# The instruction order of a two-attention kernel taken from a written list, a query tile turned by TensorE, and small sums moved to GpSimd

## The chip, the core and the metric

The kernel runs on one core of one Trainium2 chip. A core has five engines that run side by side: TensorE (PE in the profile; its weight loads are a row of their own, PEld), VectorE (DVE), ScalarE (ACT), GpSimd (POOL) and SyncE (SP), which here only issues DMAs. Each engine works through its own instructions in the order in which the program was written, and waits on semaphores where it needs another one's result. The metric is the device time of one execution in microseconds (us).

## The reference, cut to what matters

Two attention layers over 2048 tokens of width 640, 32 heads of 20; their outputs stand side by side (1280 columns).

```python
# A: four segments of 512 tokens, one after the other
for s in range(4):
    logits = einsum('bhqd,bhkd->bhqk', qs, ks) * scale + mask     # causal in the segment
    a_dot  = softmax(logits) @ vs
    pq     = phi(qs)                       # t+1 where t>0, else exp(t)
    a_mem  = (pq @ M) / (pq @ z + 1e-6)    # M, z: memory of the earlier segments
    o      = g * a_mem + (1 - g) * a_dot
    pk = phi(ks);  M += pk^T vs;  z += sum(pk)
a = concat(o) @ wo
# B: causal sliding window of 256 tokens over the same length
p = softmax(where((i - j >= 0) & (i - j < 256), q k^T * scale, -1e9))
b = (p @ v) @ wo
return concat([a, b], -1)
```

## The kernel before

The work is cut into eight chunks of 512 tokens, taken alternately: A0, B0, A1, B1, A2, B2, A3, B3. For each chunk the projections q, k, v come first (`qk_job`, `v_job`): groups of five matmuls over the 128x128 array ("wide" matmuls, helper `wide`, L870), 512 or 320 columns each, summed in one of only two PSUM banks, `m0` and `m1`. When a group is done VectorE copies it to SBUF (L501, L677, L682, L1027) and the bank is free again. Scores are made in batches (`score_batch`, L758): four heads at a time in 32-row strips of the array (the profile shows 20x128 operands), or in 32x64 pieces for half blocks; a batch fills two of three "sc" buffers of 128x1024. ScalarE then takes two exponentials per batch (L774, `pt<-sc`), which turns logits into weights; 306 of them are the bulk of its work, 18 more make phi (L521). GpSimd zeroes what the causal or window mask forbids (L813), VectorE does it for the half blocks (L791).

When the weights of a group of heads are ready, `av` (L827) or, in the last chunk, `av_tile` (L848: one tile of 128 queries, 16 heads) multiplies them with v, in 128x32 column strips, four matmuls at a time. VectorE transposes the result (`turn`, L883), and `norm` divides by the sum column: a reciprocal on VectorE (L908), a product on GpSimd (L918). For the memory term of A there is a sum with 1e-6 on VectorE first (L903, in place L906), and VectorE adds the product to `o` (L931). `final` stores `o` to DRAM with four DMAs (L949), reads it back transposed by a DMA (L968), and `final_job` multiplies it with `wo`, copies it and stores the output. Only the last query tile of the last chunk goes another way: `last_job` turns it by eight short steps of TensorE against a unit matrix (L1049, L1061), so without the trip through DRAM.

The order of all this is decided while the program is written. `Flow` keeps an estimate of when each engine is free; the main loop in `body` asks in turn whether the next score batch may go (`room`, `may_wait`), then the next attention-times-v or memory group (`pend`), then the next step of a projection (`jobs`, `fins`), takes the first that is ready by the estimate, and moves its clock on if none is. `room` holds back groups of many short matmuls once 160 of them were sent within 3000 ns of its clock. What comes out is a fixed order for each engine; nothing is decided on the chip.

Three kinds of array shape alternate on TensorE: whole array (wide), row strips (scores), column strips (attention times v).

Of the kernel before, what the change touches and what calls it, by code (L numbers as in the profile page):

```python
# [13 lines left out]
P = 128  # L14
# [14 lines left out]
FETCH = 160  # L29
FETCH_NS = 3000  # L30
BACK = 800.0
NTT = 4
QPOOL = 750.0
GAP = 48
# [20 lines left out]
LEAD = 500.0  # L55

# [11 lines left out]
class Flow:  # L68
# [3 lines left out]
    def __init__(self):  # L72
        self.pe = self.act = self.dve = self.pool = 0.0
        self.mode = None
        self.sp = self.fabric = 0.0
        self.landed = []
        self.bank_free = [0.0, 0.0]
        self.open = False
        self.left = 0
        self.later = []  # L80
        self.idle_dve = []
        self.idle_low = []
        self.blocked = []
        self.loads = []
        self.seq = 0
        self.load = {}
        self.slow = {}
        self.issued = []
# [11 lines left out]
    def room(self, n):  # L100


        while self.issued and self.issued[0][0] <= self.pe - FETCH_NS:
            self.issued.pop(0)
        have = n + sum(k for _, k in self.issued)
        t = self.pe
        for t0, k in self.issued:
            if have <= FETCH:
                break
            have -= k  # L110
            t = t0 + FETCH_NS
        return t

    def on_pe(self, mode, ns, cols, ready=0.0, n=1):
        self.issued.append((max(self.pe, ready), n))
        return self.on_pe_(mode, ns, cols, ready)
# [22 lines left out]
    def on_dve(self, ns, ready=0.0):  # L139
        self.dve = max(self.dve, ready) + ns  # L140
        return self.dve + 138.0

    def on_pool(self, ns, ready=0.0):
        self.pool = max(self.pool, ready) + ns
        return self.pool + 98.0
# [68 lines left out]
class _K:  # L214
# [29 lines left out]
    def warm_up(self):  # L244

        f = self.f
# [222 lines left out]
    def qk_job(self, n, what, pieces, w_ap, dst, needs, scratch, phi=None):  # L469
# [6 lines left out]
        if what == "k" and self.chunks[n][0] == "B":  # L476
            at = SH
            c = self.chunks[n][1]
            if 0 in pieces and c > 0:
                def prefix(t0):  # L480
                    nc.vector.tensor_copy(out=dst[:, :, 0:SH],
                                          in_=self.kB[(c - 1) % 2][:, :, L:L + SH])
                    f.on_dve(290.0)
                f.blocked.append((0.0, self.known(n - 2, "k", G - 1), prefix))
# [27 lines left out]
    def phi(self, in_, t, m, use):  # L512
# [13 lines left out]
        def one(in_, e, es, m, ta):  # L526
            box = []

            def s1():
                r = out(m)  # L530
                if r is None:
                    r, slot = self.piece("r", 1, 1)
                    box.append(slot)
                    r = r[:]
                box.append(r)
                nc.vector.tensor_scalar(out=r, in0=in_, scalar1=0.0, scalar2=1.0,  # L536
                                        op0=ALU.max, op1=ALU.add)
                f.on_dve(300.0, t)

            def s2():  # L540
                r = box[-1]
                nc.vector.tensor_tensor(out=r if len(box) == 1 else e, in0=r, in1=e, op=ALU.min)  # L542
                td = f.on_dve(370.0, ta)
# [60 lines left out]
    def dm_job(self, seg, pkT, v):  # L604
# [12 lines left out]
        for some in (own, [(lambda kt, h=h: spare[:, kt, R2 * h:R2 * h + R2], R2,  # L617
# [6 lines left out]
            for lhs, rows, xs, g0 in some:  # L624

                gs = [g0] if g0 is not None else sorted(MEM2[x][1] for x in xs)
                n = W * len(gs)
                v0 = at_head(4 * gs[0])
                for kt in range(LT):
                    nc.tensor.matmul(dM[0:rows, at:at + n], lhsT=lhs(kt),  # L630
                                     rhs=v[:, kt, v0:v0 + n],
                                     start=(kt == 0), stop=(kt == LT - 1))
                f.on_pe("full", 4 * mm_ns(n), 4 * n)
                at += n
                if (rows, xs) != (some[-1][1], some[-1][2]):
                    yield 0.0
# [148 lines left out]
    def mask(self, m, pt, te, ready, x):  # L785
        nc, f = self.nc, self.f
        kind, c0, n = m
        if kind == "ends":
            def go():
# [6 lines left out]
                ready[x] = f.on_dve(72.0 + 1.036 * n, te)  # L796
# [71 lines left out]
    def wide(self, ps, lhsT, rhs, n, start, stop):  # L868

        self.nc.tensor.matmul(ps[:, 0:n], lhsT=lhsT, rhs=rhs, start=start, stop=stop)  # L870
        self.f.on_pe("full", mm_ns(n), n)
# [16 lines left out]
    def norm(self, turned, dst, add_to, last, g=None):  # L888
# [12 lines left out]
        def s1():  # L901
            if add_to:
                nc.vector.tensor_single_scalar(out=rr[:], in_=tv[:, :, DH], scalar=EPS,  # L903
                                               op=ALU.add)
                f.on_dve(100.0, t0)
                nc.vector.reciprocal(out=rr[:], in_=rr[:])  # L906
            else:
                nc.vector.reciprocal(out=rr[:], in_=tv[:, :, DH])  # L908
            t1 = f.on_dve(276.0, t0)
            f.at(t1 - 100.0, lambda: s2(t1))  # L910

        def s2(t1):
# [14 lines left out]
            def add():  # L927
# [4 lines left out]
                t3 = f.on_dve(300.0, t2)  # L932
# [6 lines left out]
        f.when_idle(t0, s1)  # L939

    def final(self, n, o, scr, wo, out2d, r0, col, t0, t1, t):
# [19 lines left out]
        def turn(tl):  # L961
            if n not in self.oT:
# [3 lines left out]
                else:  # L966
# [7 lines left out]
                                                 lambda: box.get("t"))))  # L974

    def final_job(self, n, wo, out2d, r0, col, t0, t1, there):
# [4 lines left out]
        for tt in range(t0, t1):  # L981
            if n == len(self.chunks) - 1 and tt == LT - 2:

                row = r0 + tt * P
                for hf in range(2):
                    yield "bank"
                    self.last_half(hf, lambda m: oT[:, m, tt * P:(tt + 1) * P], wo,
                                   out2d[row:row + P], col)
                continue
# [46 lines left out]
    def last_job(self, o, wo, out2d, r0, col, t):  # L1036
# [4 lines left out]
        yield self.sc_free[-NSC]  # L1041
# [3 lines left out]
        b0 = LT * (LT - 1)  # L1045
# [6 lines left out]
        oT = [self.pq[:, 0, 0:4 * P], self.pkT[:, 0, 0:P]]  # L1052
# [12 lines left out]
        f.on_pe("col", 150.0, 128)  # L1065
# [5 lines left out]
        row = r0 + (LT - 1) * P  # L1071
# [93 lines left out]
    def job(self, gen):  # L1165
        return [gen, next(gen)]
# [29 lines left out]
    def seed(self, n):  # L1196
# [7 lines left out]
        add = lambda gen: self.jobs.append(self.job(gen))  # L1204
# [5 lines left out]
        else:  # L1210
            add(self.dm_job(c - 1, self.pkT, self.vA))
# [7 lines left out]
        for half, pieces in enumerate(((0, 1, 2), (3, 4))):  # L1219
            for some in ([(m,) for m in pieces] if first else [pieces]):  # L1220
                for what, w, dst, phi in qk:
                    need = [tx, gate] + ([self.known("wB" + what, some[0])] if first else [])
                    add(self.qk_job(n, what, some, w, dst, need, self.scr[what + kind][c], phi))
                if first and some[0] == AT:
                    add(self.late_v())
            if first:
                v[3] = v[3] + [self.known("wBv", half)]
            add(self.v_job(n, half, *v))

    def body(self, xA, A_wq, A_wk, A_wv, A_wo, A_beta, xB, B_wqkv, B_wo, out2d):  # L1230
# [84 lines left out]
        def first(what, m, dst, phi):  # L1315
# [3 lines left out]
                                     scr[what + "A"][0], phi)))  # L1319
        for m in range(KT):  # L1320
# [4 lines left out]
            if m == 1:  # L1325
                add(self.job(v(0)))
        self.late_v = lambda: v(1)
        if AT < 0:
            add(self.job(v(1)))
# [3 lines left out]
        pend = []  # L1333
# [6 lines left out]
        late = [(19500.0, self.zero_end), (45000.0, self.consts_e), (60000.0, self.consts_one)]  # L1340
        while True:
# [3 lines left out]
            if i < len(bs):  # L1345
                n, ent, ms, complete = bs[i]
                kind, c = chunks[n]
                if self.ring("pt", NPT) is not None:
# [4 lines left out]
                    if None not in need:  # L1353
                        t = max(need + [f.room(4 * len(ent)) if ent[0][1][0] in "lust" else 0.0])
                        if t <= f.pe and not self.may_wait():
# [12 lines left out]
                            for g in complete:  # L1368
                                pend.append((n, g, "tile" if n == NC - 1 else "av"))
                                if kind == "A" and c > 0:  # L1370
                                    pend.append((n, g, "mem"))
# [6 lines left out]
            if pend:  # L1378
# [6 lines left out]
                elif what == "av":  # L1385
                    ps_ = parts[(n, g)]
                    need = [whole(p[6] for p in ps_), self.done.get((n, "v", g))]
                else:
                    need = [self.done.get(("dm", c - 1)),
                            self.done.get((n, "pq", g) if g < KT else (n, "pq2"))]  # L1390
                if None not in need and not (f.open and 0 < f.left <= 3):
                    t = max(need + [min(f.bank_free), f.room(
                        4 * len(ps_)) if what != "mem" else 0.0])
                    wait = (f.mode == "full" and soon is not None and len(pend) < 3
                            and soon < f.pe + 2200.0 and self.more(f.pe))
                    if t <= f.pe and not wait:
                        pend.pop(0)
                        self.one_group(n, kind, c, g, what, parts, left, o_t, groups_done,
                                       scro, wo, out2d)
# [3 lines left out]
            for x, jb in enumerate(self.jobs + self.fins):  # L1403
                if f.open and not jb[0] is self.opener:
                    continue
# [7 lines left out]
            if hit is not None:  # L1413
                self.at_job = hit
                jb = (self.jobs + self.fins)[hit]
                if jb[1] == "bank":
                    f.open = True
                    self.opener = jb[0]
                try:
                    jb[1] = next(jb[0])  # L1420
                except StopIteration:
                    (self.jobs if jb in self.jobs else self.fins).remove(jb)
                while late and f.pe > late[0][0]:
# [15 lines left out]
        assert i == len(bs) and not pend and not self.jobs and not self.fins  # L1439
# [14 lines left out]
    def one_group(self, n, kind, c, g, what, parts, left, o_t, groups_done, scro, wo, out2d):  # L1454
# [22 lines left out]
        if what == "tile":  # L1477
# [19 lines left out]
        if what == "av":  # L1497
# [5 lines left out]
            if nm == 2:  # L1503
                self.norm(tt, o[:, :, DH * g:DH * (g + 1)], False, None)
                return
# [92 lines left out]
```

## Time and profile before

| | |
|---|---|
| median of 3 runs | 334.47 us (334.11 to 336.25) |
| the profiled execution | 334.4 us; its span from first to last instruction 331.6 us |
| granted TensorE clock | 1.000 |
| PE busy | 315.6 us (95%) |
| ACT busy | 302.4 us (91%) |
| DVE busy | 264.2 us (80%) |
| POOL busy | 256.3 us (77%) |
| first exponential starts, last one ends | 9.10 us, 318.27 us |

The span is counted by the profiler; the 2.8 us between it and the execution's time lie around the program. Matmuls overlap each other and their ends are modelled, so PE's share overstates how full it is; an engine's start-to-start times say more. ACT instructions overlap by about 0.1 us as well: four exponentials of 1024 columns that follow each other without a wait take 3.77 us, and one takes 1.02, so the next starts 0.917 us after the one before.

### The profile page before, as it was taken

The numbers are of one execution on the slowest core, as the hardware profiler recorded it, in microseconds if no ns is written. First come the engines' busy times: TensorE is split into PE (matmuls) and PEld (weight loads), VectorE is DVE, ScalarE is ACT, GpSimd is POOL, SyncE is SP. The second block draws the span as 40 slices with busy tenths as digits, with TensorE's granted clock in tenths as the row PEclk, the third lists the DMA queues.
The fourth block names the chain that finished last, engine by engine and source line by source line (L and its number), as shares of the span: only waits on it lengthen the run. The fifth ranks groups of instructions, "written<-read, shape, count | busy, mean of one in ns | idle before, by whom it ended". The sixth has DMA issues, their size and how long they took to land.

```text
span 331.6 us, 15794 instructions
## 1 busy us (share of the span) xinstructions
PE 315.6 (95%) x6583; PEld 174.4 (53%) x6619; DVE 264.2 (80%) x556; ACT 302.4 (91%) x333; POOL 256.3 (77%) x648
## 2 busy tenths in 40 slices
PE   8999999999999999989999999999999999999896
PEld 3444546455444455546644545455654545666564
DVE  6777767798978899989868898888667889876654
ACT  1979999999999999999999999989999999999841
POOL 8366689998659799975867879996875969977750
DMA  6975746566596852335699145044555154769852
GB/s 198 396 253 152 173 135 125 136 175 176 132 226 132 165 155 63 67 86 122 183 208 181 42 94 156 3 104 80 148 140 114 21 150 122 166 142 187 178 127 100
DMA packets 76260, 47.36 MB, mean 143 GB/s; under 512 B 48381, under 2 KB 73181, under 8 KB 76189
## 3 DMA queue, kind: packets, MB, share of 16 engines
q1 hardware_dynamic: 75469, 45.71, 56.7%
q8 instruction: 51, 0.84, 1.1%
q10 hardware_dynamic: 720, 0.66, 0.7%
q14 instruction: 20, 0.16, 0.2%
HBM read 17.62 MB, written 16.96 MB: 104 GB/s over the span
## 4 chain that ended last, share of the span: by engine, by line
PE 57%; DVE 15%; ACT 10%; issue 7%; POOL 6%; DMA 3%; SPq 1%; ACTq 0%; DVEq 0%; POOLq 0%
PE m L870 36%; PE sc L758 11%; ACT pt L774 10%; PE m L827 6%; POOL pt L813 4%; DVE pt L791 4%; PE m L848 2%; DVE tt L883 2%; POOL u L918 2%; DVE pq L542 2%; DVE kA L501 2%; DVE vA L677 1%; DMA xT<-in_A_x_dram 1%; DVE pq L536 1%; DVE ot L1027 1%
## 5 line engine op out<-in xcount | busy, mean ns | idle before, releaser
L774 ACT ACTIVATE pt<-sc 128x1024 bf16<-128x1024 f32 (+2 forms) x306 | 285.0, 1012 | 10.7 <-PE sc L758 8.6
L813 POOL TENSOR_SCALAR_AFFINE_SELECT pt<-pt 128x128 bf16<-128x128 bf16 (+1 forms) x512 | 177.1, 374 | 60.4 <-ACT pt L774 57.4
L883 DVE STREAM_TRANSPOSE tt<-m 128x512 f32<-128x512 f32 x88 | 61.4, 711 | 20.0 <-PE m L827 9.1
L918 POOL TENSOR_TENSOR o<-tt,rr 128x320 bf16<-128x320 f32 x64 | 47.8, 747 | 4.1 <-DVE rr L908 4.0
L870 PEld LDWEIGHTS <-xT 128*128 128x128 bf16 x350 | 32.0, 97 | 24.2 <-issue 12.3
L758 PE MATMUL sc<-qB,kB 20*64 20x64 bf16 (+2 forms) x1728 | 38.6, 218 | 1.4 <-issue 0.8
L791 DVE TENSOR_TENSOR pt<-pt,ends 128x1024 bf16<-128x1024 bf16 (+2 forms) x50 | 36.3, 740 | 0.0
L758 PEld LDWEIGHTS <-kB 20*64 20x64 bf16 (+1 forms) x1728 | 21.7, 98 | 23.3 <-issue 22.0
L758 PE MATMUL sc<-qA,kA 20*64 20x64 bf16 (+4 forms) x1024 | 33.1, 237 | 0.5
L1027 DVE CAST ot<-m 128x320 bf16<-128x320 f32 x56 | 26.9, 485 | 7.4 <-PE m L870 7.1
L870 PEld LDWEIGHTS <-oT 128*128 128x128 bf16 x280 | 24.7, 98 | 11.4 <-issue 1.1
L870 PE MATMUL m<-wBv,xT 128*128 128x320 bf16 x160 | 27.0, 299 | 2.4 <-DVE tt L883 2.3
L870 PE MATMUL m<-wv_A,xT 128*128 128x320 bf16 x160 | 26.0, 299 | 2.0 <-DVE vA L677 1.9
L870 PE MATMUL m<-xT,wBq 128*128 128x512 bf16 x96 | 26.4, 381 | 0.4 <-issue 0.2
L870 PE MATMUL m<-xT,wq_A 128*128 128x512 bf16 x88 | 25.0, 381 | 1.8 <-DVE vA L677 0.8
L870 PE MATMUL m<-xT,wk_A 128*128 128x512 bf16 x96 | 25.6, 388 | 1.1 <-DVE qA L501 0.7
L870 PE MATMUL m<-xT,wBk 128*128 128x512 bf16 x84 | 24.8, 381 | 0.8
L758 PEld LDWEIGHTS <-kA 20*128 20x128 bf16 (+1 forms) x1024 | 13.5, 97 | 20.6 <-issue 19.6
L827 PE MATMUL m<-pt,vA 128*32 128x192 bf16 (+3 forms) x512 | 23.6, 275 | 0.0
L870 PE MATMUL m<-wo_A,oT 128*128 128x320 bf16 x140 | 22.7, 300 | 0.2
L501 DVE CAST kB<-m 128x512 bf16<-128x512 f32 x20 | 13.8, 691 | 9.4 <-PE m L870 9.4
L870 PE MATMUL m<-wo_B,oT 128*128 128x320 bf16 x120 | 19.4, 300 | 0.3 <-DVE ot L1027 0.3
(112 smaller groups left out, 405.3 us busy)
## 6 DMA issues: line engine op xcount, KB each, us to landing
out_dram<-ot SPq DMA_DIRECT2D x29, 160.0 KB
scr_o<-o SPq DMA_DIRECT2D x28, 160.0 KB
xT<-in_B_x_dram SPq DMA_DIRECT2D x8, 288.0 KB
xT<-in_A_x_dram SPq DMA_DIRECT2D x8, 256.0 KB
scr_pk<-e SPq DMA_DIRECT2D x15, 128.0 KB
vS<-vA SPq DMA_DIRECT2D x16, 87.0 KB
vL<-vB SPq DMA_DIRECT2D x8, 174.0 KB
scr_kA<-kA SPq DMA_DIRECT2D x16, 60.0 KB
```

The lines of the kernel that those rows point to most:

```text
L501: nc.vector.tensor_copy(out=dst[:, m, at:at + L], in_=ps[:, :])
L542: nc.vector.tensor_tensor(out=r if len(box) == 1 else e, in0=r, in1=e, op=ALU.min)
L758: nc.tensor.matmul(ps[j // 2][h0:h1, j % 2, c0:c0 + nq], lhsT=k[rows, g, k0:k0 + h1 - h0], rhs=q[rows, g, q0:q0 + nq], start=True, stop=Tr ...
L774: nc.scalar.activation(out=pt[:, :, lo:hi], in_=ps[i][:, :, lo:hi], func=ACT.Exp, scale=self.scale)
L791: nc.vector.tensor_tensor(out=blk, in0=blk, in1=self.ends[:, c0, :].unsqueeze(1).unsqueeze(1) .to_broadcast([P, 2, n // SH, SH]), op=ALU.mult)
L813: nc.gpsimd.affine_select(out=blk, in_=blk, pattern=pat, compare_op=ALU.is_ge, fill=self.zero, base=base, channel_multiplier=mul)
L827: nc.tensor.matmul(O[HD * j:HD * j + HD, q0:q0 + nq], lhsT=v[:, at_head(h):at_head(h) + HD], rhs=pts[j // 2][:, j % 2, c0:c0 + nq], start= ...
L848: nc.tensor.matmul(O[HD * j:HD * j + HD, o0:o0 + nq], lhsT=v[:, at_head(h):at_head(h) + HD], rhs=pts[j // 2][:, j % 2, c0:c0 + nq], start= ...
L870: self.nc.tensor.matmul(ps[:, 0:n], lhsT=lhsT, rhs=rhs, start=start, stop=stop)
L883: self.nc.vector.transpose(out=tt[:], in_=O[:, :])
L918: nc.gpsimd.tensor_tensor(out=to[:] if add_to else to, in0=a, in1=b, op=ALU.mult)
L1027: nc.vector.tensor_copy(out=ot[:, 320 * hf:320 * hf + 320], in_=ps[:, 0:320])
```

## The change

1. **The order is read from a list.** `PLAN` is a string of tokens: `S` or `s` is a score batch, `A` an attention-times-v group, `M` a memory group, and `k00*5` five wide matmuls of the job named k00 (what, chunk, first piece); `o..` are output projections, `v..` v projections, `d..` memory sums, `z0`, `z1` the jobs of the last two query tiles. Each job now has its label, and the main loop takes only what the list names next, and waits for it by its clock where it isn't ready. `room` and the rule of 160 in 3000 ns are gone; `Flow` instead counts 256 TensorE instructions to a block and 3900 ns from block to block. Several durations of `Flow` are changed, and it lets VectorE and GpSimd hold each other up; that shifts only the order in which their instructions are written.
2. **Wide matmuls between a capital `S` and the next batch, where an `A` stands among them, are split** into four column strips, so that they have the shape of the attention-times-v matmuls beside them: 192 wide matmuls (102 of 512 columns, 90 of 320) become 768.
3. **The third query tile of the last chunk** goes the way of the fourth, through `last_job` (token z0), instead of the trip through DRAM.
4. **The sum with 1e-6** (24 of them, 128x16 each) moves from VectorE to GpSimd, as a step `s0` ahead of the reciprocal.
5. The memory groups have a queue of their own (`memq`) instead of standing behind their attention group in `pend`.

```diff
+PLAN = (
+    "k00*5 q00*5 k01*4 S k01 q01*5 S v00*16 S v00*4 k02 S k02*4 k03*5 q02*3 S q02*2 q03*5 k04*5 "
+    "A S A q04*5 v01 s v01*9 s k10*5 S v01*10 S q10*2 A S q10*3 q11*3 S q11*2 q12*5 A s k11*5 "
...
+    "M v70*9 s v70 A M s q73*2 M q73*3 s k73*5 q73*2 s q73*3 A s o30*5 M s v71*5 A s M v71*5 "
+    "o30*4 s o30 A M s v71*8 s v71*2 A M s o30*9 s o30 o40*5 o30*5 s o30*5 A s o40*10 s o40*15 "
+    "A s o40*5 o50*5 s o40*5 o50*5 s A o50*4 s o50*6 s A o50*4 s o50*8 s o50*8 s A o60*5 s "
+    "o60*10 o70*5 s A o70*3 s o70*2 o60*7 s o60*8 o71*2 s o71*3 o60*2 A o60*3 z0 o71*5 o60 A "
+    "o60 z0 o60*3 z0 z1*2 z0 z1*2 ")
...
-                        t = max(need + [f.room(4 * len(ent)) if ent[0][1][0] in "lust" else 0.0])
-                        if t <= f.pe and not self.may_wait():
+                        t = max(need)
+                        if t <= f.pe and (want or not self.may_wait()):
+                            if want:
+                                plan.pop()
...
     def wide(self, ps, lhsT, rhs, n, start, stop):
 
-        self.nc.tensor.matmul(ps[:, 0:n], lhsT=lhsT, rhs=rhs, start=start, stop=stop)
-        self.f.on_pe("full", mm_ns(n), n)
+        f = self.f
+        if self.by_tiles:
+            for j in range(4):
+                s = slice(HD * j, HD * j + HD)
+                self.nc.tensor.matmul(ps[s, 0:n], lhsT=lhsT[:, s], rhs=rhs, start=start,
+                                      stop=stop, tile_position=(0, HD * j),
+                                      skip_group_check=True)
+            f.on_pe("col", n / 2.4 + COL_NS, n, 0.0, 4)
+        else:
+            self.nc.tensor.matmul(ps[:, 0:n], lhsT=lhsT, rhs=rhs, start=start, stop=stop,
+                                  skip_group_check=True)
+            f.on_pe("full", mm_ns(n), n)
...
-        def s1():
+        def s0():
+            nc.gpsimd.tensor_single_scalar(out=rr[:], in_=tv[:, :, DH], scalar=EPS, op=ALU.add)
+            t = f.on_pool(EPS_NS, t0)
+            f.when_idle(t, lambda: s1(t))
+
+        def s1(te=None):
             if add_to:
-                nc.vector.tensor_single_scalar(out=rr[:], in_=tv[:, :, DH], scalar=EPS,
-                                               op=ALU.add)
-                f.on_dve(100.0, t0)
                 nc.vector.reciprocal(out=rr[:], in_=rr[:])
...
                 if g0 == G - 4:
-                    if qt == LT - 1:
-                        self.fins.insert(0, self.job(self.last_job(o, wo["end"], out2d, c * L, col, t)))
+                    if qt >= LT - 2:
+                        self.fins.insert(0, self.job(self.last_job(
+                            o, wo["end"], out2d, c * L, col, t, qt), "z%d" % (qt - LT + 2)))
                         return
```

Read from the written program: TensorE has 14,432 instructions instead of 13,240. The shape of the array changes 340 times instead of 382 from one matmul to the next. The number of exponentials, masks, transposes and reciprocals is the same; ScalarE has one copy more.

More of the change, by code (lines that the diff above doesn't have):

```diff
@@ L87, in __init__ @@
         self.slow = {}
-        self.issued = []
+        self.sent, self.block, self.starved = 0, 0.0, 0.0
+        self.dve_at, self.pool_at = [], []
+        self.count = 0
     def full_rate(self, t):
@@ L981, in final_job @@
         for tt in range(t0, t1):
[L982 to L989, printed above, removed]
             while self.ring("ot", NOT) is None:
@@ L1340, in body @@
         late = [(19500.0, self.zero_end), (45000.0, self.consts_e), (60000.0, self.consts_one)]
+        plan = PLAN.split()
+        plan = [x.split("*")[0] for x in plan for _ in range(int((x + "*1").split("*")[1]))]
+        visits, tiles = [False], False
+        for x in plan:
+            if x in "Ss":
+                visits.append(False)
+                tiles = x == "S"
+            elif x == "A" and tiles:
+                visits[-1] = True
+        plan.reverse()
+        over = set()
         while True:
```

177 lines of the change are left out of this document (120 added, 57 removed), and 15 rows, old and new, of the table PLAN.

## The prediction

> **What bounds the kernel now.** First the windows by stage, then ScalarE's row by shape, the chain of waits at the end, the waits and the DMA queues.
>
> ```profile
> core 0: us, PE busy (x) PEld busy (x) DVE busy (x) ACT busy (x) POOL busy (x), PEclk, DMA share, GB/s
> 0.00:9.10 9.10, 8.00 (x31) 2.85 (x32) 5.19 (x8) 2.10 (x5) 6.75 (x30) 1.00 0.72 217
> 9.10:285.00 275.90, 265.36 (x5427) 142.85 (x5463) 229.77 (x489) 267.12 (x291) 221.01 (x553) 1.00 0.56 138
> 285.00:318.30 33.30, 32.06 (x982) 21.67 (x980) 23.34 (x49) 31.36 (x34) 26.31 (x62) 1.00 0.79 167
> 318.30:331.60 13.30, 10.19 (x148) 7.03 (x145) 5.92 (x13) 1.81 (x4) 2.21 (x4) 1.00 0.45 124
> ```
>
> Between the first and the last exponential (9.10 to 318.27, 309.2 us) ACT is busy 97% and 94% of two stages; before and behind it has nearly nothing. So three pieces make the span: 9.1 of lead, 309.2 at ACT's pace, 13.35 of tail.
>
> ```profile
> 314.49 3.77 ACT L774 ACTIVATE pt<-sc 128x1024 bf16<-128x1024 f32 x4 [0.95 <-PE sc L758]
> ```
>
> An exponential costs (3.77 - 1.02) / 3 = 0.917 us start to start. With 284 of these, 20 of 768 columns at 0.704, two of 512 at 0.494, 12 phi at 0.946 and six at 0.53 (their records' start to start), ACT needs 290.0 us; 309.2 - 290.0 = 19.2 us are stalls. I followed the records of each stall over 0.06 us (81 of them). In 21, 8.4 us together, TensorE had waited in the stretch before: for a bank that DVE had not emptied (5.6), for a GpSimd mask (1.7), or for instructions (1.05). The other 60 (10.8 us) had no such wait: between two score batches TensorE had more matmuls than the two exponentials last.
>
> ```profile
> PE m L870 <- DVE vA L677: 2.7, 4, 0.8
> PE m L870 <- DVE tt L883: 2.3, 12, 0.2
> PE m L870 <- DVE qA L501: 1.1, 3, 0.5
> ```
>
> These waits are ordered by DVE's queue, not by its load: the 2.7 us are four events of up to 0.8.
>
> ```profile
> 311.56 1.47 PE m L870 x10
> 313.02 0.16 PE sc L758 x3
> 313.18 0.84 issue
> 314.02 0.39 PE sc L758 x13
> 314.41 1.47 PE m L870 x10
> 315.88 0.34 PE sc L758 x16
> 316.21 0.83 PE m L848 x64
> ...
> 323.05 0.22 PE sc L1049 x4
> 323.27 0.23 PE sc L1061 x12
> 323.50 5.00 PE m L870 x35
> ...
> 328.53 0.49 DVE oe L1087
> ```
> ```profile
> q8 instruction: 51, 0.84, 1.1%
> ```
>
> A batch with ten wide matmuls, 1.47 + 0.34 = 1.81, just matches two exponentials (1.83): the last chunk runs balanced. And TensorE stops for 0.84 us inside a batch without a semaphore. That is at its instruction 12,740. The q8 queue brings 16 KB packets, one per 13,257 / 51 = 260 instructions (256, the first block being there), and each starts when TensorE passes number 196 + 256k; 12,740 is the 49th such place. Between such places it never took less than 3.66 us; the block before the stop took 3.9.
>
> **Part by part.** Sums are against the profiled execution, 334.4 us (span 331.6 + 2.8), which lies at the median of the three runs (334.47).
>
> *Tail.* The third tile's detour goes: four stores and a transposing DMA on SP (issues of 3.22 us from 314.08 and 1.21 us at 318.59), so SP's queue is shorter at the end and nothing is put before others. TensorE gets eight more steps for it (0.22 + 0.23). What it does after the last score shrinks from 11.55 to 7.8 us at start-to-start prices; the 3.7 us of output projections come earlier. Then the chain of the last tile decides, not TensorE's backlog. Its last attention matmul ends at 320.2 as now (it needs the masks, ending 319.13). In the rows of the last tile the transpose ends 0.9 later, the product on GpSimd 2.0 later (322.2); the turn and its copy took 1.35 from its start (322.88 to 324.22), so 323.6; then ten wide matmuls (1.36), 0.3 to the copy, 0.49 of copy and 2.6 to the span's end: 328.4 against 331.6. Gain 3.2 us. If the last matmul needs only the last masks and ends at 319.6, 3.8; if one projection half (0.68) blocks the turn, 2.5.
>
> *The list.* I went through the 152 stretches from one score batch to the next in both written orders, gave each matmul its record's start to start (wide 512: 0.216, 320: 0.136, 0.096 more where the shape changes; a strip group of four, 128 to 320 columns: columns / 2.4 ns + 3) and set the sum against ACT's exponentials in that stretch, where TensorE may be one exponential ahead, because there are three sc buffers. In the old order TensorE is over by more than 0.5 us in 5 stretches; in the new one in 14. One can be read off the list: in `s o40*15 A s`, 15 wide matmuls, 64 strips and a batch, 1.47 + 0.68 + 0.83 + 0.34 = 3.3 us by the chain's rows against 1.83. Carried along the order, with 0.29 us from matmul to exponential, ACT runs dry for 9.1 us in the old order (measured: 10.8) and 14.9 in the new one. So the list alone costs 5.7 us; with the shortest hand-over that rows show (0.20) 5.3 and 11.0, the same difference. The 42 changes of shape that go (4.0 us of TensorE) and the 3.7 us that come from the tail are in this.
>
> *Splitting.* The trace has no strips of 512 columns. The rows nearest: strip groups of 320 and of 256 at columns / 2.4 + 2.7 ns, so 216 ns and no cost; the first group after a change pays 10 to 13 ns more. Bounds for 102 groups of 512: 0 to 1.3 us; I take 0.
>
> *Instructions.* 1,192 more come to TensorE in the middle of the run. At ACT's pace 10 of the new order's 55 blocks take under 3.9 us, the shortest 2.4. Against the 3.66 that the trace shows as possible 3.0 us are missing, against 0.7 in the old order. Part lies where ACT is ahead: between 0 and +2.3, I take 0 because the longest one lies beside the 15 wide matmuls counted above. [...]
>
> *1e-6 sums.* 24 x 0.371 = 8.9 us leave DVE (264 busy). GpSimd has no such row; nearest are its products of 128x20 (0.232) and selects of 128x128 (0.305): 5.6 to 7.3 us in 24 places, hidden in its 23% of idle time. If that cover is gone, the masks queued behind the sum wait (it waits for DVE's transpose), and the attention matmuls for the masks: 24 x 0.3 = 7 at most; below, it can give up to 2.0, the wait of TensorE's loads for DVE's L906. I take 0 here, and let the DVE time show in the next term.
>
> *The other waits.* Of the 8.4 us behind DVE, masks and fetch the list may remove all (its lumps lie where they are) or none (it is as fixed as the old order). I take three quarters, 6.3, since three causes move at once: DVE is lighter, memory groups no longer stand in line with attention groups, and TensorE has wide matmuls to fill with. What is late next is the stretches above.
>
> Sum: 334.4 - 3.2 + 5.7 - 6.3 = 330.6.
>
> **Rivals.**
>
> *Lumps where waits were.* The 5.7 and the 8.4 are the same time: long stretches stand where ACT would have starved for DVE. Old stalls at 214, 217 and 223 us (0.76, 0.61, 0.68) have new lumps close by. For it: half of 5.7 counted, all of 8.4 gone: 334.4 - 3.2 + 2.8 - 8.4 = 325.6. Against: the old stretches there fitted well.
>
> *The gain is eaten.* Only 3 of the 8.4 go: 334.4 - 3.2 + 5.7 - 3 = 333.9. For it: banks are still two, and a group waits for the copy two groups back.
>
> *Slower: the list lets ACT run dry.* TensorE holds to a list made for other durations, none of the 8.4 goes and fetch adds 2.3: 334.4 - 3.2 + 5.7 + 2.3 = 339.2. It decides where a stretch exceeds 1.83 us without ACT being ahead, and it wins over the tail from 3.2 us of lost ACT time on. For it: 14 stretches against 5, and the balanced last chunk now has lumps of 1.3 and 0.6.
>
> *The change does less than it says.* Excluded from the orders: TensorE's follows the list to its end, only two transposing loads of tiles are left, all 24 sums stand on GpSimd.
>
> **How the numbers follow.** Forecast case 330.6, chance 0.36; lumps on waits 325.6, 0.20; eaten 333.9, 0.24; slower 339.2, 0.20. What a measurement can tell from no change is about 1%, 331.1 to 337.8. The forecast lies near that edge: its own range, 326.8 (nine tenths of the 8.4, 3.8 of tail, a third of the 5.7 hidden) to 332.6 (5.0 of the 8.4, 2.5 of tail), puts 0.30 below and 0.06 within. Faster 0.50, same 0.29 (0.06 + 0.22 of eaten + 0.01), slower 0.21. The range goes from 324 to 339: one tenth below 325.6's case, one tenth above the slower one.
>
> **What would show it.** Tail: the last exponential's end to the span's end 10.2 instead of 13.35, and no row of L870 x35 in the chain. List: ACT's first start to last end, 309.2 now, at 308 to 310; 330.6 means 308.5. Waits of L870 for DVE under 3 us (6.1 in the three rows above). Fetch: issue pauses over 0.3 us inside batches, at 196 + 256k. Sums: GpSimd rows of 128x16 near 0.23 us. It is wrong if ACT's stretch falls under 304 (then the list is better than stretch sums say) or rises over 312.

## The result and the profile after

The changed kernel takes 332.67 us (median of 16 runs, 331.91 to 334.00) beside 334.27 us for the kernel before on the same chip: ratio 0.9957, 95% interval 0.994 to 0.9973. That is 1.6 us less, within 1%; 3.8 us less had been forecast. The profiled execution took 333.1 us; it is one of four of the 16 with a mean granted clock of 0.994 or less, and its clock was halved for a while in the long stage (below). Cut at the first and last exponential, as the prediction cuts it:

| us | before | forecast | after |
|---|---|---|---|
| lead, to the first exponential | 9.10 | 9.1 | 8.76 |
| first to last exponential | 309.17 | 308.6 | 311.75 |
| tail, last exponential to span's end | 13.35 | 10.15 | 10.90 |
| outside the span | 2.8 | 2.8 | 1.7 |
| profiled execution | 334.4 | 330.6 | 333.1 |

The windows by stage of the kernel after, columns as before (length; busy us and instructions of PE, PEld, DVE, ACT, POOL; granted clock; DMA share; GB/s):

```profile
8.76:285.00 276.24, 269.66 (x6043) 147.88 (x6043) 221.94 (x465) 262.74 (x289) 226.35 (x570) 0.99 0.59 142
285.00:320.51 35.51, 35.02 (x1014) 23.32 (x1012) 26.00 (x53) 32.98 (x36) 29.95 (x69) 1.00 0.67 149
320.51:331.40 10.89, 6.37 (x135) 4.10 (x132) 4.13 (x9) 2.07 (x6) 2.24 (x4) 0.92 0.19 62
```

ACT still has to do the same work and now needs 2.6 us more for it. PE is busier in the long stage (269.7 us, on the split matmuls) and not in the tail. The clock in the long stage is no longer 1.00; the 0.92 of the last stage comes from the end, where the trace's clock records have TensorE at half clock from 329.8 us on, with nothing left for it to do.

From the table of waits (waiter, releaser: us in all, times, longest):

```profile
ACT pt L830 <- PE sc L814: 12.7, 22, 2.1
DVE vA L733 <- DMA vS<-vA: 2.2, 1, 2.2
PE m L883 <- DVE vA L733: 1.7, 1, 1.7
ACT e L577 <- DVE kA L557: 1.7, 1, 1.7
PE m L935 <- DVE tt L949: 0.8, 4, 0.3
```

TensorE's own waits that the prediction wanted gone are mostly gone: of the three rows of L870 behind VectorE, 6.1 us, the 0.8 in the last row and 0.3 more are left (L870 is L935 now), and all waits of PE's matmuls for DVE in that table add up to 3.0 us instead of 7.5. But 1.7 of the 3.0 is a single wait that was not there before. Its source is the row above it: VectorE itself waited 2.2 us for a DMA. ACT's waits for scores, 8.6 us in 20 before, rose to 12.7: what TensorE no longer waits did not reach ScalarE (counted out below, where the forecast is gone through).

That one wait, in the timeline (start us, length, engine, line, instruction, count, and in brackets the idle time before it and its releaser), with rows of SyncE's queue, VectorE, TensorE and ScalarE in order of time:

```profile
72.75 2.52 SPq L319 DMA_DIRECT2D wo_B<-in_B_wo_dram  x2
75.36 1.33 SPq L757 DMA_DIRECT2D vS<-vA  x2
...
79.82 0.49 DVE L733 TENSOR_TENSOR vA<-m,omg 128x320 bf16<-128x320 f32 x1 [2.22 <-DMA vS<-vA]
...
80.37 0.29 PE L883 MATMUL m<-pt,vX 128*32 128x256 bf16 x4 [1.74 <-DVE vA L733]
...
82.26 1.06 ACT L577 ACTIVATE e<-kA 128x1024 bf16<-128x1024 bf16 x1 [1.66 <-DVE kA L557]
```

`vS<-vA` copies the first half of v to a second layout. VectorE may not write vA again before that copy has read it. In the kernel before, SyncE issued the copy first and the weights wo_B, which nobody needs yet, behind it:

```profile
73.10 1.69 SPq L701 DMA_DIRECT2D vS<-vA  x2
...
76.18 1.38 SPq L263 DMA_DIRECT2D wo_B<-in_B_wo_dram  x2
```

In the changed kernel the two have changed places: 2.52 us of issuing stand ahead of the copy. VectorE stops, then TensorE, which waits for the bank, then ScalarE, 1.66 us. How long VectorE's wait is differs between executions: with the same order of these issues it is 2.0 us in the traces of e2 and e3, 1.2 in those of e6 and e8, and there is none in e7's, where the issue of wo_B took 0.92 us. And the clock, in windows of 1 us (the last three columns are clock, DMA share and GB/s):

```profile
79.00:80.00 1.00, 0.00 (x0) 0.00 (x0) 0.18 (x1) 1.00 (x2) 0.00 (x0) 1.00 0.62 112
80.00:81.00 1.00, 0.63 (x22) 0.59 (x25) 0.96 (x4) 0.60 (x1) 0.44 (x1) 0.79 0.40 80
81.00:82.00 1.00, 1.00 (x96) 0.91 (x84) 1.00 (x2) 0.00 (x0) 1.00 (x3) 0.50 0.00 0
82.00:83.00 1.00, 0.98 (x28) 0.58 (x13) 1.00 (x4) 0.74 (x1) 0.85 (x3) 0.50 0.41 122
83.00:84.00 1.00, 1.00 (x5) 0.48 (x4) 0.78 (x3) 1.00 (x2) 0.76 (x1) 0.50 0.42 138
```

Behind the empty microsecond TensorE gets half its clock for 3.41 us (the length of the clock's record in the trace). ScalarE stands still once more behind it, 0.91 us at 86.05; e3's execution, with nearly the same wait and the full clock, has no such gap there.

The longest of the stretches that the prediction read off the list, `s o40*15 A s`, in the chain of waits (start us, us, what):

```profile
291.79 2.21 PE m L935 x15
294.00 0.80 PE m L904 x63
294.80 0.55 PE sc L814 x53
295.34 0.28 issue
295.62 0.34 PE sc L814 x11
```

2.21 + 0.80 + 0.89 of scores and 0.28 of a stop for instructions: ACT's exponential behind it started 2.18 us late. Other such lumps stand where the list has them, by the records of ACT's stalls: 1.36 at 211.1, 1.19 at 17.5.

The end of the same chain:

```profile
325.00 1.48 PE m L935 x10
326.50 0.43 ACT oe L1149
326.95 0.35 ACTq L1156
327.48 0.69 ACT ot L1074
```

TensorE's 35 wide matmuls are gone from it. The last piece is a copy, `ot`, whose last matmul had ended at 323.36: the list takes `o60*3` as single steps, and the eviction behind the third is a step of its own, written when the list has ended and so behind both copies of the last tile (L1149) in ScalarE's order.

### The profile page after: what moved, and what is told of

Same layout as the page of the kernel before. It is cut to its first block, busy times and chain, and to the rows that moved or that the text cites. A ratio compares the mean times of both kernels' runs of the same rounds, so it can differ in the third digit from the quotient of the medians.

```text
span 331.4 us, 17005 instructions
## 1 busy us (share of the span) xinstructions
PE 318.7 (96%) x7215; PEld 178.1 (54%) x7215; DVE 257.3 (78%) x534; ACT 299.9 (90%) x334; POOL 265.3 (80%) x672
## 4 chain that ended last, share of the span: by engine, by line
PE 52%; DVE 7%; ACT 5%; issue 4%; POOL 3%; DMA 2%; SPq 0%; POOLq 0%; ACTq 0%; DVEq 0%
PE m L935 28%; PE sc L814 11%; PE m L883 7%; PE m L930 5%; ACT pt L830 4%; DVE tt L949 3%; PE m L904 1%; POOL pt L869 1%; DMA scr_pk<-e 1%; DMA vL<-vB 1%; POOL o L987 1%; DVE kA L557 1%; DVE pt L847 1%; DVE qA L557 1%; DVE o L1000 0%
## 5 line engine op out<-in xcount | busy, mean ns | idle before, releaser
L830 ACT ACTIVATE pt<-sc 128x1024 bf16<-128x1024 f32 (+2 forms) x306 | 282.9, 1024 | 14.6 <-PE sc L814 12.7
L814 PE MATMUL sc<-qB,kB 20*64 20x64 bf16 (+2 forms) x1728 | 40.1, 219 | 1.0 <-ACT pt L830 0.5
L935 PEld LDWEIGHTS <-xT 128*128 128x128 bf16 x286 | 25.7, 97 | 17.1 <-issue 6.2
L935 PEld LDWEIGHTS <-oT 128*128 128x128 bf16 x244 | 21.7, 98 | 11.3 <-issue 1.3
L935 PE MATMUL m<-wBv,xT 128*128 128x320 bf16 x147 | 24.2, 299 | 1.0 <-DVE tt L949 0.4
L935 PE MATMUL m<-xT,wBq 128*128 128x512 bf16 x82 | 21.4, 380 | 0.4 <-DVE tt L949 0.3
L935 PE MATMUL m<-wo_A,oT 128*128 128x320 bf16 x125 | 21.2, 307 | 0.1
L935 PE MATMUL m<-xT,wBk 128*128 128x512 bf16 x81 | 20.9, 380 | 0.0
L935 PE MATMUL m<-wv_A,xT 128*128 128x320 bf16 x119 | 20.0, 300 | 0.1
L738 DVE CAST vB<-m 128x320 bf16<-128x320 f32 x32 | 15.6, 486 | 4.7 <-PE m L935 2.4
L557 DVE CAST qB<-m 128x512 bf16<-128x512 f32 x20 | 13.8, 688 | 6.5 <-PE m L930 3.2
L935 PE MATMUL m<-wo_B,oT 128*128 128x320 bf16 x109 | 18.6, 300 | 0.0
```

What stands on the lines that cost most here:

```text
L557: nc.vector.tensor_copy(out=dst[:, m, at:at + L], in_=ps[:, :])
L738: nc.vector.tensor_copy(out=dst, in_=src)
L814: nc.tensor.matmul(ps[j // 2][h0:h1, j % 2, c0:c0 + nq], lhsT=k[rows, g, k0:k0 + h1 - h0], rhs=q[rows, g, q0:q0 + nq], start=True, stop=Tr ...
L830: nc.scalar.activation(out=pt[:, :, lo:hi], in_=ps[i][:, :, lo:hi], func=ACT.Exp, scale=self.scale)
```

## The experiments

The profiled execution of each gives the stretch from first to last exponential and the tail; times are medians, ratios are against the kernel before in the same session. The medians of the kernel before in these sessions lie between 333.5 and 334.3 us, so small differences between rows are better read from the ratios.

| | time us | ratio (95%) | exponentials | tail |
|---|---|---|---|---|
| after | 332.67 | 0.9957 (0.994 to 0.9973) | 311.75 | 10.90 |
| e1_turn_alone | 334.42 | 0.9999 (0.9979 to 1.002) | 309.96 | 13.79 |
| e2_even_last_chunk | 336.63 | 1.0078 (1.0052 to 1.0103) | 314.63 | 12.72 |
| e3_copy_at_once | 331.30 | 0.9903 (0.9874 to 0.9931) | 311.58 | 10.28 |
| e4_no_list | 335.13 | 1.0043 (1.0022 to 1.0063) | 313.63 | 11.28 |
| e5_sums_on_dve | 332.19 | 0.994 (0.9916 to 0.9964) | 311.93 | 10.82 |
| e6_no_splitting | 334.11 | 1.0013 (0.9989 to 1.0036) | 313.67 | 10.91 |
| e7_even_border_moved | 333.84 | 1.0005 (0.9981 to 1.003) | 309.39 | 12.72 |
| e8_border_at_end | 332.34 | 0.9953 (0.9925 to 0.9981) | 311.83 | 10.88 |
| e9_copy_before_load | 330.93 | 0.9906 (0.9878 to 0.9933) | 309.89 | 10.90 |
| e10_copies_and_load | 330.03 | 0.9883 (0.9857 to 0.9909) | 309.13 | 10.28 |
| e11_and_even_moved | 331.63 | 0.9935 (0.9907 to 0.9962) | 309.75 | 10.71 |
| e12_all_and_sums | 329.34 | 0.9877 (0.9846 to 0.9907) | 308.46 | 10.20 |

**e1_turn_alone**: the kernel before, with only part 3 of the change.

```diff
-                    if qt == LT - 1:
+                    if qt >= LT - 2:
                         self.fins.insert(0, self.job(self.last_job(...
```

> The kernel before with the third query tile of the last chunk turned by TensorE and nothing else; its order is still found while the program is written. Long-stretch theory (the list's uneven stretches cost the exponentials what the tail gains): all of the tail's gain stays, so the first to last exponential takes 309.2 us as before (within 0.7), the tail 10.2 to 11.0 instead of 13.35, time 330.3 to 331.5 (ratio 0.988 to 0.992), faster than the change's 332.67. That holds with 1.1 us outside the span gone, since this program does not end at a place where a block of instructions is fetched; without that 331.4 to 332.6. Rival (the list is worth as much as the tail): 332.5 or more, since the turn puts work of the old tail into the stretch of the exponentials.

The tail did not shrink (13.79). With no list the main loop puts 30 output projections behind the turns, and the chain ends in the kernel's old way:

```profile
325.74 4.21 PE m L870 x30
...
329.97 0.49 DVE ot L1019
```

The time lies in the rival's range, but not for its reason: the stretch grew by only 0.8 us. So the turn by itself gives nothing here; the tail shrinks only where those projections are also called earlier. That doesn't take the list: e4 below has an empty one, but the changed main loop and its changed durations, and its tail is 11.28.

**e2_even_last_chunk**: the list's last three lines spread evenly (`s o40*10 s o40*5 A s o40*10 s o40*10 s A o50*5 ...` in place of `s o40*10 s o40*15 A s ...`).

> The change with its list evened out in the last chunk alone: no stretch between two score batches has more than ten output matmuls, or five beside an attention group; the 15 beside an attention group, which stood ahead of a stall of 2.18 us, become five. Long-stretch theory: the stall at 296 us falls under 0.6, the one at 313 us under 0.3, first to last exponential 311.7 to about 309.5 to 310.2, time 330.8 to 331.5 (ratio to before 0.990 to 0.992). Rival (instructions come too slowly there, the 15 matmuls only filled that wait): the stall turns into pauses of TensorE without a semaphore of 1 us or more inside a batch, time 332.4 to 333.

336.63 us, 5 us above the forecast and 3.6 above the rival's range. Where the 15 matmuls had been, TensorE now stops with no semaphore at its instruction 12,740 = 196 + 256 x 49, for 2.25 us from start to start, of which 2.04 are idle:

```profile
296.76 0.21 PE L815 MATMUL sc<-qB,kB 20*64 20x64 bf16 x1 [2.04 <-issue]
```

The lump was real, but it had also covered a stop at a border of a block, as the rival said. 0.9 us behind the stop the clock is halved for 3.41 us: ten wide matmuls there, from 299.54, take 2.20 us to the next scores instead of 1.47. This is a second loss that neither branch had.

**e7_even_border_moved**: the same list, and three wide warm-up matmuls replaced by 60 tiny ones.

```diff
+                for _ in range(20):
+                    self.nc.tensor.matmul(ps[0:HD, 0:HD], lhsT=ones(HD), rhs=ones(HD),
+                                          start=True, stop=True)
```

> The evenly spread last chunk again (336.6), with 60 tiny matmuls instead of 3 wide ones in the warm-up before any data is there, so that all borders between blocks of 256 TensorE instructions lie 114 instructions earlier in the work. Theory (the stop of 2.25 us belongs to where a border falls): no stop over 0.8 us in the last 40 us, time 334 to 335. Rival (the dense stretch outruns the supply wherever its border lies): stops of 1.5 us and more stay between 285 and 318, time 336 to 337.

The long stop is gone and 2.8 us with it, and so is the half clock behind it; stops of 1.04 at 312.4 and about 0.7 at 304.4 (start to start) are left. The theory asked for none above 0.8, so it holds for the place and not for the whole. ScalarE's stretch is 2.4 us shorter than that of the changed kernel, yet the time is not: the tail is longer, with two late copies in it. The 2.4 us are no measure of the even list either: this profiled execution (332.78, the lowest of the 12) has no wait for the copy out of vA, and taking that wait from the changed kernel (e9) shortens the stretch by 1.9 us. What an even list saved in this chunk depended on where a border falls (a stop of 2.25 us in e2, none over 1.04 in e7), which no list shows.

**e3_copy_at_once**: the eviction written in the same step as its last matmul.

```diff
-                        yield 0.0
+                        if hf == 0 or m < self.KT - 1:
+                            yield 0.0
```

> The change with one copy written where its matmuls end: the eviction of the last tile that two score buffers hold (ACT 128x640 in the tail) is put right behind its last matmul instead of behind the last token of the list. Theory (the end of the tail is that copy and its DMA, behind two copies that had waited for TensorE): the copy starts near 323.5 instead of 327.5 us, the last DMA issue is VectorE's half tile, span 0.3 to 1.0 us less, ratio to before 0.992 to 0.995. Rival (the landing of the half tiles sets the end anyway): 0.9957 as now, within 0.001.

The copy `ot` stands at 323.33 instead of 327.48, and the tail is 10.28 instead of 10.90. The ratio, 0.9903, is lower than the forecast's 0.992 to 0.995: the median falls by 1.4 us, more than the 0.62 of the tail. All six executions have a clock of 0.999 or more; what else is in the rest is open.

```profile
324.93 2.22 PE m L935 x15
...
327.18 0.49 DVE oe L1153
```

**e4_no_list**: the changed kernel with an empty `PLAN`, so that the main loop chooses again, and nothing is split.

> The change with an empty list: the order is found while the program is written, by the changed rules and durations; no wide matmul is split then, the turn of the third tile and the sums on GpSimd stay. Stretch sums by the rows: TensorE over by more than 0.5 us in 7 stretches (14 with the list, 5 before), ScalarE dry for 12.7 us (14.9, 9.1). Long-stretch theory: first to last exponential 309.5 to 311.5, time 331 to 332.5, as fast as with the list or faster. Rival (the list is what keeps the other waits down): 333.5 or more.

With an empty list the time is 2.5 us longer (335.13 against 332.67), 1.9 of it in the exponentials' stretch, although the list's stretch sums let ACT run dry longer (14.9 us against 12.7). But an empty list also splits nothing. e6 below has the list without splitting: its stretch, 313.67, is that of e4, 313.63, and its time is 1.0 us lower, with overlapping intervals of the ratios. So the order alone gains nothing in the stretch, and what e4 loses there splitting can account for. Against the stretch sums of e6 (16.6 us) the list's order does remove some 3.9 us of other waits; about 2 of these are stops at block borders, which add up to 3.3 us in e4 (1.18, 1.34 and 0.78, start to start) and to 1.23 in e6. The tail, 11.28, is nearly that of the list: 2.1 of its 2.5 us of gain come without one. Which of the changed rules and durations does it was not separated.

**e6_no_splitting**: `if False and self.by_tiles:` in `wide`.

> The changed kernel with the 192 wide matmuls whole, so 1,152 TensorE instructions fewer and 394 instead of 340 changes of shape (54 x 0.096 = 5.2 us of TensorE). Theory (splitting pays by its shapes): the stretch sums let ScalarE run dry for 16.6 instead of 14.9, so 334 to 335. Rival (splitting costs what its instructions cost in fetching): the 1.8 us of stops at block borders fall under 0.6, and the time is 331.5 to 332.5.

The theory holds: the stretch grows by 1.9 us, where the sums said 1.7. With 1,152 instructions fewer one stop of 1.23 us (start to start) for instructions stayed, at 308.7, so that did not remove the stops either.

**e5_sums_on_dve**: the sum with 1e-6 back in front of the reciprocal on VectorE.

> The changed kernel with its 24 sums with 1e-6 back on VectorE; TensorE's order is the same. The question is why the waits behind VectorE did not go. Theory (the order sets them, not VectorE's load): within 1 us of the changed kernel's 332.7, ScalarE's stretch 311 to 313, VectorE busy 257 + 24 x 0.255 = 263.5, and the stalls behind VectorE's banks at 8 us as before. Rival (the moved sums are what kept those waits from growing under the list): 334.5 to 337, with the stalls behind VectorE above 10 us. If GpSimd's sum instead delays the masks, it becomes faster, 331 to 332.

332.19, no difference outside the intervals. TensorE's waits for VectorE are 3.9 us with the sums on VectorE and 3.0 without: the load of 24 x 0.26 us isn't what sets the time. ScalarE's stalls behind such waits are 7.6 us instead of 4.8 (counted as in the next part), but all its stalls together are 23.2 and 23.1.

**e8_border_at_end**: 44 matmuls of two columns behind the last one, into a scratch bank.

> The changed kernel with 44 matmuls of two columns behind its last one, so that a 57th block begins five instructions before TensorE's end, as the 52nd does in the kernel before. Theory (the chip still fetches that block before the execution ends): the part outside the span grows from 1.7 to 2.8 as in the kernel before, span 330.5 to 332.5 as in the changed kernel's runs, time 333.5 to 334.5. Rival (the 1.1 us have another cause): it stays at 1.7, time 332 to 333.5.

Not settled. The part outside the span was 1.66 to 1.92 us in nine of the ten executions and 3.08 in one; the kernel before has 1.67 to 3.37 with a median near 1.95, and the changed kernel 1.70 to 1.77 in all 16. So a border near the end went with a long part in one of e8's executions and in some of before, as in the profiled one (2.8: its last packet of the queue q8 starts at 333.44, 1.8 us behind the span's end), and isn't a cost of 1.1 us each time.

**e9_copy_before_load**: the load of wo_B is allowed only when the copy of vA is issued.

```diff
-        wo["B"] = self.load_w("wo_B", B_wo[0], self.known(2, "q", 3), 6000.0)
+        wo["B"] = self.load_w("wo_B", B_wo[0], self.known(2, "v", 0), 6000.0)
```

> The changed kernel; only the load of wo_B is issued six places later on SyncE's queue, behind the copies vS<-vA and the stores of qA. In the changed kernel VectorE waits 2.22 us at 77.6 us for the copy out of vA, because the list calls the v projection there and the load of wo_B (2.52 us of issuing) went ahead of the copy; TensorE then stands for 1.74 us, ScalarE loses 1.66 at 82.3 and 0.91 at 86, and in half of the executions the granted clock is 0.5 to 0.8 for 4 us behind it. Theory (this one wait is what my forecast of the other waits misses): the wait falls under 0.5, ScalarE's stretch goes from 311.7 to 308.5 to 310, no execution is below a clock of 0.997, time 330 to 331.3. Rival (ScalarE's lost time there is made up later, where it would have waited anyway): 332 to 333.

TensorE's order is the same, instruction by instruction; two issues on SyncE have moved. (The expectation's half of the executions was too many: four of 16 of the changed kernel have a clock of 0.994 or less.) The timeline of e9, rows of SyncE, VectorE and ScalarE in order of time:

```profile
74.23 1.72 SPq L757 DMA_DIRECT2D vS<-vA  x2
...
77.79 0.48 DVE L733 TENSOR_TENSOR vA<-m,omg 128x320 bf16<-128x320 f32 x1
...
78.36 0.89 SPq L319 DMA_DIRECT2D wo_B<-in_B_wo_dram  x2
...
80.68 1.14 ACT L577 ACTIVATE e<-kA 128x1024 bf16<-128x1024 bf16 x1
```

VectorE writes vA at 77.79 with no wait, ACT's step follows at 80.68 instead of 82.26, all six executions have a clock of 0.997 or more, and the time falls by 1.7 us (ratio 0.9906 against 0.9957, intervals apart). The rival, that ACT would have waited anyway, is out. The edit takes away the wait and the half clock that followed it in the changed kernel's profiled execution. The 12 executions of the changed kernel above a clock of 0.994 have a median of 332.4 us, so by this estimate some 0.3 of the 1.7 us are the clock's and 1.4 the wait's.

**e10_copies_and_load** (e3 and e9 together), **e11_and_even_moved** (with e7's list and warm-up as well) and **e12_all_and_sums** (e10 with the sums on VectorE):

> The same edit on top of the eviction that is written right behind its last matmul (331.3). If the two gains add, 328.7 to 330, and this beats both kernels by over 1%; if the second one is made up in the last chunk, 330.5 to 331.5.

> The same two edits, with the evenly spread last chunk and its moved block borders. That one ended ScalarE's stretch 2.2 us earlier than the changed kernel (318.3) but had two late copies at the end (tail 12.7). If the early eviction repairs the tail to 10.5, 327.5 to 329.5; if GpSimd's masks and products set the end of the last chunk (they stand in its chain from 307 to 321), no better than the kernel beside it.

> The fastest kernel so far (the early eviction and the load of wo_B behind the copy of vA, 330.03), with the 24 sums with 1e-6 back on VectorE. With the sums alone put back, 332.2 against 332.7 left it open whether GpSimd's 24 x 0.266 us cost anything, because the two intervals overlap. If the sums cost on GpSimd what they delay its masks by, 328.3 to 329.5 here, and ScalarE's stretch under 308.7 (309.1). If it is the same on both engines, 329.6 to 330.5.

With both repairs the time is 330.03, 1.2% under the kernel before and 0.8% under the changed one. That is just outside the first branch's 328.7 to 330, and under the 1% that it asked for against the changed kernel: 2.6 us, where the repairs one by one give 1.4 and 1.7. In the profiled executions the stretch is 2.6 and the tail 0.6 shorter than the changed kernel's. The even last chunk is by medians still the worse one with them (the intervals just touch): its chain goes through GpSimd's masks and waits for them from 304.7 to 319, as the second branch said, its profiled execution has stops for instructions of 1.42 us at 230.1 and 1.11 at 312.7, and four of its 12 executions have a clock of 0.995 or less, the cause of which is open. Where the sums stand stays open: e12 is 0.7 us under e10 by medians, as its first branch said, but its ratio is the same within the intervals.

## Why the forecast missed

**What bounds the kernel, and the cut in three:** borne out. In every kernel above the span is ACT's stretch with a lead and a tail, and repairs of either show in the time.

**The other waits, -6.3:** this is the step that failed. The term stood for stalls of ScalarE behind a wait of TensorE, 8.4 us. Counted over the records by the prediction's rule, with its prices, the kernel before has 82 stalls of 19.5 us (the prediction: 81 of 19.2), 8.5 of it behind a wait for VectorE, a mask or instructions; the changed kernel has 57 stalls of 23.1 us, 9.2 behind such a wait. So none of the 6.3 came. TensorE's waits for VectorE did become fewer, 3.0 us instead of 7.5, but those that are left stand beside long stretches, and the stall is as long: one of 2.2 us at 295.94 holds a wait of only 0.28. Charged to the wait only as far as the wait lasts, 6.4 us became 4.2, a gain of 2.2.

What the step left out is what a new order adds: "what is late next is the stretches above". What was late next was, in good part, a copy of vA that the new order put behind 2.52 us of weight loads on SyncE, while the list calls the next v projection just then. e9 takes that away and nothing else: 1.7 us of the time, where the forecast is 2.1 us short of the measured time and 3.1 us short of the measured span. With it the stretch and the tail are 309.89 and 10.90 against a forecast of 308.6 and 10.15. The rest of what the term lacked is not traced to causes one by one. The orders of both kernels were there to be compared on SyncE's queue, too.

**Tail, -3.2:** right in kind, too large: -2.45 measured. Of the 0.75 that is missing, e3 shows 0.62 to be the eviction that the list leaves for its end. The step looked at TensorE's and SyncE's order there, not at ScalarE's. And the gain was put down to the turn; e1 shows that the turn alone gives none, and e4 that with the changed main loop most of it comes without the list.

**List, +5.7:** right in kind; its size depends on the count. ScalarE's stalls with no wait in front rose by 2.9 us (11.1 to 13.9); where a wait is charged only for its own length, what remains for long stretches rose by 5.7 (13.1 to 18.9). The lumps stand where the sums have them; e6 moves the stretch by 1.9 where the sums say 1.7. e2 shows a limit: the lump that it removed uncovered a stop for instructions (2.25 us).

**Splitting 0, sums 0:** the sums, yes (a median of 0.266 us each on GpSimd where 0.23 was estimated, no effect that runs can tell). Splitting saves 1.4 us by e6, which the forecast had counted in the list's term by the changes of shape; the stretch sums agree, 1.7.

**Instructions, 0 (to +2.3):** the stops of TensorE at 196 + 256k are not 0. From start to start the larger ones add up to 1.7 us after (0.80, 0.42 and 0.49), against 1.06 before; as idle time to about 1.0 against 0.84. In the changed kernel's trace blocks took as little as 2.85 us, so 3.66 wasn't the limit. In e2 a single one is 2.25 us.

**Outside the span:** 2.8 was carried over as fixed. It is 1.7 after, and near 1.95 in the median of before, so 1.1 us in the table and some 0.2 in the medians came from a place without a term. The forecast of the span alone (327.8) therefore missed by 3.1 us of 330.95 (median), and e9's 329.2 is 1.4 above it. With e3's repair as well (e10) it is 328.4, 0.6 above. For the rest in the stretch, 309.9 against 308.6 in e9, stops for instructions are a candidate: four of them make 1.8 us of idle time in its trace against 0.84 before. No run separates it.

**The rivals:** "the gain is eaten" (333.9) came nearest, in the number and in the mechanism, waits that stay; but they are largely not the old ones. "Slower" counted the right new costs, lumps and stops. By ScalarE's stalls even its premise that none of the 8.4 goes is near the truth, but on top of that its 339.2 took 5.7 for long stretches, which by the same count grew by 2.9, and 2.3 for stops that grew by less than 1 us. "Lumps where waits were" has one such place, at 294 us, where e2 found a wait under the lump; nothing was gained by it.

## What to carry to other kernels

When a change rewrites an order, compare every queue's order, the DMA queue's as well: for each transfer that moved back, ask which engine next overwrites what it reads, and when (e9: two issues moved, 1.7 us of the time). Where steps are taken from a list, write an eviction together with its last matmul, or it lands wherever the list ends (e3: the copy 4.15 us earlier, the tail 0.62 us shorter). And the balanced stretch sums were no gain by themselves: stops for instructions (2.25 us in e2) and waits for GpSimd's masks (304.7 to 319 in e11) took the room.

## What the runs showed of the hardware

In three profiled executions a short stop of TensorE was followed by half its clock. In the changed kernel 1.74 us of waiting were followed, 0.2 us later, by 3.41 us at a granted clock of 0.50; in e5, after a stop of 1.43 us until 79.96, the same 3.41 us began at 82.3; in e2, 0.9 us after the stop of 2.04. It isn't certain: e3's profiled execution kept 1.00 after 1.51 us. The 12 executions of the changed kernel above 0.994 have a median of 332.4 us, the other four 333.5. What decides whether half the clock follows a stop was not shown.

The larger stops of TensorE with no semaphore came at whole blocks of 256 of its instructions (196 + 256k), but not at the same ones in each kernel. Instruction 12,740 stops before, after, e2, e3, e4, e5, e8 and e9, by 0.32 to 2.25 us from start to start; in e1 and e6 there is next to nothing there, and their stops lie at other borders (0.93 us at 11,972 in e1, 1.23 at 12,228 in e6). Moving the work by 114 instructions (e7) took the longest, e2's 2.25 us, away; 1.04 is the longest that it has in the last 40 us. In the traces of before and after, the three of them with over 0.25 us of idle time ended 1.41 to 1.52 us behind the end of a 16 KB packet of the queue q8, `instruction` (at 314.02 behind 312.50 before; at 162.40 behind 160.99 and at 295.62 behind 294.16 after). That these stops are waits for instructions is the author's reading of this and of their places.
